# Gate and up products of a transformer block's MLP by Strassen's scheme: seven products over half tiles in place of eight

## The chip, the cores and the metric

The kernel runs on one NeuronCore of one Trainium2 chip. The metric is the device time of one launch in microseconds (us); lower is better. The kernel before took 2897.82 us, the median of three runs (2895.48 to 2900.39).

The engines named below: PE (TensorE, matrix products into PSUM banks), DVE (VectorE), ACT (ScalarE), POOL (GpSimd) and SP (SyncE, which here only issues DMAs). Each works off its own queue in order and waits on semaphores for the others.

## The reference, cut to what matters

```python
def _A_ref(x, wqkv, wo):          # B=1, S=2048, D=576, H=32 heads of 18
    ...
    p = _softmax(scores, axis=-1)
    ...
def _B_ref(x, w_gate, w_up, w_down):   # 576 -> 4608 -> 576
    g = jnp.einsum("bsd,df->bsf", x, w_gate)
    u = jnp.einsum("bsd,df->bsf", x, w_up)
    h = _gelu(g) * u
    return jnp.einsum("bsf,fd->bsd", h, w_down)

x = A_x
h = x + _A_ref(_layernorm(x, axis=-1), A_wqkv, A_wo)
h2 = h + _B_ref(_layernorm(h, axis=-1), B_w_gate, B_w_up, B_w_down)
```

All inputs are float32. The kernel computes products of float32 matrices from float16 parts: each operand is a high and a low part, and a product is high x high + low x high + high x low, so three float16 matmuls for each 128 rows of the contraction.

## The kernel before, in words

**Attention.** The first half, up to about 1560 us, is attention in units of four heads and 512 query rows, numbered n = 0 to 31, with 16 steps (kt) each. Row maxima run on DVE ahead of the exponentials on ACT. In the last three units, when the maxima run out, two generators are stepped beside the attention: `fill` multiplies the attention output by `wo` for one block of 512 rows (`wo_block`, L675), normalizes those rows and splits them into float16 parts, and `turn` (L231) transposes the parts into `XT` by DMA; `side` prepares the first weights of the MLP.

**MLP.** The width of 4608 is worked off in nine chunks of 512. `XT` holds the normalized rows, transposed: the 576 rows of the contraction are four tiles of 128 (high in `xh`, low in `xl`) and a tail of 64, whose high and low parts share one tile (`xt`). So one output tile of 128 wide by 512 rows takes 4 x 3 + 2 = 14 matmuls with 512 moving columns (`products`, L264, `accumulate`, L273). `gate_up` (L745) does that for gate and for up, for four tiles of the width and for one block of rows. ACT applies gelu out of the gate's bank (L756), DVE multiplies with the up bank (L759), ACT rounds to a high part (L760), DVE takes the low part (L761). `down` (L765) then multiplies the 512 wide hidden tile by the chunk of `w_down` in groups of 12 matmuls with 288 moving columns, and DVE adds each group onto `nat` (L779). Four PSUM banks serve the gate and up tiles, four the groups of `down`.

**Weights.** While chunk c is multiplied, the three pieces of chunk c+1 are loaded (`load_gate_up`, `load_down`: six and one DMAs on SP), their largest magnitudes are found (`exponents`, L113 on: DVE reduces over the free axis, PE transposes the column of 128 maxima at L131, DVE reduces again at L133, PE spreads the result over all partitions at L138), a power of two is made of it, and ACT and DVE split the weights into high and low parts (L252, L255, L739, L740). Two slots hold the split weights of two chunks. The loads have their own float32 buffers (`gf`, `uf`, `df`).

**Order of the work.** Up to the end of attention the order on PE, ACT, DVE and POOL is the program's own (`manual_schedule`), and generators are stepped with `take`. After `in_order.close()` (L865) a scheduler places the instructions of the MLP; the order on each engine is fixed at build time either way.

Of the kernel before, what the change touches and what calls it, by code (L numbers as in the profile page):

```python
# [2 lines left out]

# [14 lines left out]
P = 128  # L18
# [12 lines left out]
def tile_block(  # L31
# [27 lines left out]
    FT = 4  # L59
    FC = FT * P  # L60
    NCH = DF // FC
    QK = 2 * D
# [19 lines left out]
    down_ring = ring(singles)  # L82

# [32 lines left out]
    def exponents(views, name):  # L116
# [3 lines left out]
        ac = small.tile([P, n, k], F32, tag=f"ac{n}", name=f"ac_{name}")  # L120
# [67 lines left out]
    def rstd_of(t0, nt, root=False):  # L188
# [16 lines left out]
        for k in (1024.0,) if root else (1.0, 1.0, 1024.0):  # L205
# [463 lines left out]

    GU = 2 * 4 * (NK + 1) * FC  # L670
    xbs = [view(A, GU + 4 * HALF * i, (HALF,)) for i in range(3)]
    y = view(WK, 2 * 4 * TB * NPE, (D,))
    ys = [view(V, GU + 4 * FT * D + 2 * L * i, (L,), F16) for i in range(2)]

    def wo_block(b):  # L675

        for t in range(b * TPB, (b + 1) * TPB):
            for i in range(2):
                ws = slice(i * HALF, (i + 1) * HALF)
                xb = xbs[(2 * t + i) % 3]  # L680
                nc.sync.dma_start(xb, xv[:, t, ws])
                pt = next(m_ring)
# [5 lines left out]
        rstd_of(b * TPB, TPB)  # L688
        for t in range(b * TPB, (b + 1) * TPB):
            normed(y, nat[:, t], t)  # L690
            if b == 0:
                split_rows(ys[t % 2], y, nc.gpsimd.tensor_copy, nc.gpsimd.tensor_sub)
            else:
                split_rows(ys[t % 2], y, nc.vector.tensor_copy if b < NB - 1 else nc.scalar.copy)
            turn(ys[t % 2], t)
            yield


    slots = []
    for region in (V, W):  # L700
        t = [view(region, 2 * (NK + 1) * FC * i, (NK + 1, FC), F16) for i in range(4)]
        t += [view(region, GU + 2 * FT * D * i, (FT, D), F16) for i in range(2)]
        slots.append(t)
    hts = [[view(WK, 2 * FT * TB * (2 * i + k), (FT, TB), F16) for k in range(2)]
           for i in range(2)]
    ghost = {"h": 0}
    gf = view(A, 0, (NK + 1, FC))
    uf = view(A, GU // 2, (NK + 1, FC))
    df = view(V, GU + 4 * FT * D, (FT, D))

    def load_gate_up(c, eng=nc.sync):
        fs = slice(c * FC, (c + 1) * FC)
        load_w(gf, w_gate[:, fs], eng)
        load_w(uf, w_up[:, fs], eng)

    def split_gate_up(c, hi_on=None):

        gh, gl, uh, ul, _, _ = slots[c % 2]
        e = yield from exponents([gf, uf], "gu")
        s = pow2(e, -1, 268, "s_gu")  # L720
        gsc = pow2(e[:, 0:1], 1, -24, "gsc")
        hsc = pow2(e[:, 0:1], -1, 224, "hsc")
        yield from split_w(gf, s[:, 0:1], gh, gl, hi_on)
        yield from split_w(uf, s[:, 1:2], uh, ul, hi_on)
        return e, gsc, hsc

    def load_down(c, eng=nc.sync):
        eng.dma_start(df, w_down[c * FC : (c + 1) * FC, :].rearrange("(c p) n -> p c n", p=P))

    def split_down(c, e):  # L730

        dh, dl = slots[c % 2][4:]
        ed = yield from exponents([df], "dn")
        s = pow2(ed, -1, 268, "s_dn")
        nc.vector.tensor_add(ed, ed, e[:, 0:1])
        nc.vector.tensor_add(ed, ed, e[:, 1:2])
        dsc = pow2(ed, 1, -262, "dsc")
        for f in range(FT):
            nc.scalar.activation(dh[:, f], df[:, f], AF.Copy, scale=s)  # L739
            nc.vector.scalar_tensor_tensor(dl[:, f], df[:, f], s, dh[:, f],  # L740
                                           op0=ALU.mult, op1=ALU.subtract)
            yield
        return dsc

    def gate_up(c, b, gsc, hsc):  # L745

        gh, gl, uh, ul, _, _ = slots[c % 2]
        sl = slice(b * TB, (b + 1) * TB)
        hh, hl = hts[ghost["h"] % 2]
        ghost["h"] += 1  # L750
        for f in range(FT):
            ws = slice(f * P, (f + 1) * P)
            pg, pu = next(single_ring), next(single_ring)
            run(accumulate(pg[:, :TB], [(q, a) for a, q in products(sl, gh, gl, ws)]))
            ga = small.tile([P, TB], F32, tag="tmp", name="ga", bufs=3)
            nc.scalar.activation(ga, pg[:, :TB], AF.Gelu_apprx_tanh, scale=gsc)  # L756
            yield
            run(accumulate(pu[:, :TB], [(q, a) for a, q in products(sl, uh, ul, ws)]))
            nc.vector.scalar_tensor_tensor(ga, pu[:, :TB], hsc, ga, op0=ALU.mult, op1=ALU.mult)  # L759
            nc.scalar.copy(hh[:, f], ga)  # L760
            nc.vector.tensor_sub(hl[:, f], ga, hh[:, f])  # L761
            yield
        return hh, hl

    def down(c, b, h, dsc):  # L765
        hh, hl = h
        dh, dl = slots[c % 2][4:]
        for i in range(TPB):
# [140 lines left out]
```

## Time and profile before

| | us |
|---|---|
| median of three runs | 2897.82 |
| lowest, highest | 2895.48, 2900.39 |
| span of the profiled execution | 2899.4 |
| PE busy, share of the span | 2752.8, 95% |
| DVE busy | 1942.0, 67% |
| ACT busy | 1432.5, 49% |
| POOL busy | 321.8, 11% |
| largest group of the first half: row maxima on DVE (L532) | 1265.0 |
| products with 512 moving columns (L278), x2240 and x2044 | 491.4, 447.4 |

The only time of the profiled execution that the profile states is its span; it is 1.6 us above the median of the runs. In the rows of the profile "x" is the number of instructions, "busy" their time together, "mean ns" the time of one. Matmuls overlap in the pipeline, so the mean of one matmul is longer than the distance between two of them. A row of the timeline gives start and length in us, and in brackets how long the engine had been idle and who released it. "SPq" is SP's queue, where DMAs are issued.

### The profile page before, as it was taken

Reading aid. Unit: us, or ns where it says so; the run is one execution under the profiler, and the core shown is the slowest. Engines: PE = TensorE matmul, PEld = TensorE weight load, DVE = VectorE, ACT = ScalarE, POOL = GpSimd, SP = SyncE. Lnnn points to the kernel's source line nnn. Section 1 sums busy time; section 2 is a strip of 40 time slices with the busy share of each in tenths; the row PEclk is TensorE's granted clock in tenths of the full one; section 3 lists DMA queues with packets and bytes.
Section 4 is the critical chain, followed back from the end, with each engine's and each line's share of the span. In section 5 each row is a group of like instructions: output and inputs, shape, how many; then the busy total and the mean of one; then the engine's idle time right before and its main releaser. Section 6 shows DMA issues by size and latency. Waiting matters only on the chain.

```text
span 2899.4 us, 42932 instructions
## 1 busy us (share of the span) xinstructions
PE 2752.8 (95%) x17178; PEld 1152.0 (40%) x17178; DVE 1942.0 (67%) x3485; ACT 1432.5 (49%) x1626; POOL 321.8 (11%) x484
## 2 busy tenths in 40 slices
PE   7999999999999999999887999999999999999999
PEld 3542222222222222222223555555555555555555
DVE  6369999999999999999864725252525252524222
ACT  4217888888888888888563312121212121212111
POOL 2102421222212221212100000000000000000000
PEclk9999999999999999999998999999999999999999
DMA  8211110101001010101113301010101010100001
GB/s 216 67 58 39 40 35 14 38 14 32 14 18 34 14 38 12 35 14 50 40 45 93 96 1 53 1 53 1 53 1 53 1 53 1 53 1 1 1 17 50
DMA packets 109404, 105.08 MB, mean 36 GB/s; under 512 B 61780, under 2 KB 79828, under 8 KB 109204
## 3 DMA queue, kind: packets, MB, share of 16 engines
q1 hardware_dynamic: 102964, 89.98, 11.0%
q0 software_dynamic: 5712, 11.19, 1.4%
q8 instruction: 134, 2.20, 0.3%
q10 hardware_dynamic: 528, 1.18, 0.1%
q14 instruction: 66, 0.54, 0.1%
HBM read 72.09 MB, written 14.42 MB: 30 GB/s over the span
## 4 chain that ended last, share of the span: by engine, by line
PE 50%; DVE 43%; ACT 3%; DMA 2%; issue 1%; SPq 1%; POOL 0%; POOLq 0%; DVEq 0%; ACTq 0%
DVE mx L532 40%; PE pair L278 32%; PE bank L278 16%; PE bank L582 1%; PE bank L529 1%; ACT W L252 1%; ACT V L252 1%; DMA X<-V 0%; ACT V L739 0%; PE pair L576 0%; ACT W L739 0%; DMA X<-A 0%; ACT WK L578 0%; DMA A<-qk_hi 0%; DVE st L185 0%
## 5 line engine op out<-in xcount | busy, mean ns | idle before, releaser
L532 DVE TENSOR_REDUCE mx<-bank 128x1 f32<-128x512 f32 x2048 | 1265.0, 683 | 28.6 <-PE bank L529 28.5
L578 ACT ACTIVATE WK<-pair,p_ex_sc 128x1024 f32<-128x1024 f32 x1024 | 1084.6, 1113 | 235.8 <-PE pair L576 234.8
L582 PE MATMUL bank<-WK,V 128*32 128x512 f32 x4096 | 549.7, 608 | 0.1
L278 PE MATMUL pair<-X,V 128*128 128x512 f16 x2240 | 491.4, 381 | 8.8 <-ACT ga L756 8.6
L278 PE MATMUL pair<-X,W 128*128 128x512 f16 x2044 | 447.4, 379 | 1.5 <-ACT ga L756 1.5
L759 DVE SCALAR_TENSOR_TENSOR ga<-pair,p_hsc,ga 128x512 f32<-128x512 f32 x144 | 107.8, 749 | 506.3 <-PE pair L278 500.6
L278 PEld LDWEIGHTS <-WK 128*128 128x128 f16 x3456 | 338.1, 98 | 93.8 <-issue 0.5
L756 ACT ACTIVATE ga<-pair,p_gsc 128x512 f32<-128x512 f32 x144 | 98.8, 686 | 483.4 <-PE pair L278 483.4
L278 PEld LDWEIGHTS <-W 128*128 128x128 f16 x2296 | 223.7, 98 | 284.5 <-issue 13.6
L529 PE MATMUL bank<-W 54*128 54x512 f16 x1024 | 291.5, 382 | 43.1 <-DVE mx L532 14.1
L278 PEld LDWEIGHTS <-V 128*128 128x128 f16 x2240 | 219.4, 98 | 271.4 <-issue 14.8
L529 PE MATMUL bank<-A 54*128 54x512 f16 x1024 | 279.4, 382 | 36.0 <-DVE mx L532 6.1
L760 ACT CAST WK<-ga 128x512 f16<-128x512 f32 x144 | 88.9, 618 | 436.9 <-DVE ga L759 436.9
L779 DVE SCALAR_TENSOR_TENSOR nat<-bank,p_dsc,nat 128x288 f32<-128x288 f32 x288 | 147.7, 516 | 196.8 <-PE bank L278 196.8
L582 PEld LDWEIGHTS bank<-WK,V 128*32 128x32 f32 x4096 | 81.3, 108 | 434.4 <-issue 406.3
L278 PE MATMUL bank<-V,WK 128*128 128x288 f16 x1920 | 239.5, 286 | 0.2 <-DVE nat L779 0.2
L278 PE MATMUL bank<-W,WK 128*128 128x288 f16 x1536 | 191.4, 286 | 0.0
L576 PE MATMUL pair<-W 56*128 56x512 f16 x1024 | 159.3, 379 | 6.0 <-ACT WK L578 5.4
L576 PE MATMUL pair<-A 56*128 56x512 f16 x1024 | 156.5, 377 | 1.6 <-ACT WK L578 0.8
L761 DVE TENSOR_TENSOR WK<-ga,WK 128x512 f16<-128x512 f32 x144 | 99.3, 690 | 78.1 <-ACT WK L760 77.9
L605 POOL TENSOR_TENSOR rp<-rc,minus_one 128x16 f32<-128x16 f32 x28 | 81.9, 2924 | 616.3 <-DMA rc<-nat 616.3
L529 PEld LDWEIGHTS <-W 54*128 54x128 f16 x1024 | 59.3, 93 | 222.0 <-issue 220.0
(170 smaller groups left out, 1276.9 us busy)
## 6 DMA issues: line engine op xcount, KB each, us to landing
V<-in_B_w_down_dram SPq DMA_DIRECT2D x8, 1152.0 KB
nat<-rc SPq DMA_DIRECT2D x32, 256.0 KB
A<-in_B_w_gate_dram SPq DMA_DIRECT2D x8, 1024.0 KB
A<-in_B_w_up_dram SPq DMA_DIRECT2D x8, 1024.0 KB
qk_hi<-qk SPq DMA_DIRECT2D x36, 128.0 KB
qk_lo<-qk SPq DMA_DIRECT2D x36, 128.0 KB
A<-in_A_x_dram SPq DMA_DIRECT2D x32, 144.0 KB
out_dram<-nat SPq DMA_DIRECT2D x16, 288.0 KB
```

The costliest lines, as they stand in the source:

```text
L278: nc.tensor.matmul(dst, a, b, start=(i == 0), stop=(i == len(pairs) - 1))
L529: nc.tensor.matmul(pms[j][:, :TB], Q[r, q0 : q0 + P], K[r, kc * TB : (kc + 1) * TB], start=True, stop=True)
L532: nc.vector.tensor_reduce(mx[:, t, 2 * pr + j, kc : kc + 1], pms[j][:, :TB], axis=AX.X, op=ALU.max)
L576: nc.tensor.matmul(pS[:, j, :TB], K[r, kt * P : (kt + 1) * P], Q[r, qc * TB : (qc + 1) * TB], start=True, stop=True)
L578: nc.scalar.activation(pes[(2 * kt + pr) % NPE], pS[:, :, :TB], AF.Exp, scale=ex_sc)
L582: nc.tensor.matmul(acc[32 * hh : 32 * hh + 32, :TB], Vg[n // NB][:, kt * G4 + hh * VC : kt * G4 + hh * VC + 32], pes[(2 * kt + hh // 2) % ...
L605: nc.gpsimd.tensor_tensor(rc, den, minus_one.to_broadcast([P, R]), op=ALU.pow)
L756: nc.scalar.activation(ga, pg[:, :TB], AF.Gelu_apprx_tanh, scale=gsc)
L759: nc.vector.scalar_tensor_tensor(ga, pu[:, :TB], hsc, ga, op0=ALU.mult, op1=ALU.mult)
L760: nc.scalar.copy(hh[:, f], ga)
L761: nc.vector.tensor_sub(hl[:, f], ga, hh[:, f])
L779: nc.vector.scalar_tensor_tensor(nat[:, t, ws], pt[:, :HALF], dsc, nat[:, t, ws], op0=ALU.mult, op1=ALU.add)
```

## The change

Strassen's scheme (in Winograd's form) multiplies two matrices that are cut in halves both ways with seven products of halves in place of eight, at the price of sums of halves before and after. Here the weights of 576 by 256 are cut into four pieces of 288 by 128 (A11, A12, A21, A22, with the sums S1 to S4), and the rows of two blocks of 512 by 576 into four pieces of 512 by 288 (B11, B21, B22 and B12, with the sums T1 to T4). Per pair of width tiles and pair of row blocks, for gate and for up, seven products of 7 matmuls each (288 = 2 x 128 + 32: 2 x 3 matmuls, and one for the tail of 32, whose three part products are stacked in 96 rows) replace eight halves of 7 matmuls.

What goes with it:

- Chunks are 256 wide; there are 18, taken in pairs (`sc`), with one `w_down` piece of 512 by 576 per pair. A `unit(c, p)` is one chunk and one pair of row blocks: 14 products (seven for gate, seven for up, in turn), with the banks of one product continued by another. Besides gelu, multiply, high and low, DVE adds (L892, L896, L915, L920, L934, L939) and ACT copies banks to temporaries (two for each sum), so a unit has 14 operations on DVE and 14 on ACT for its four hidden tiles; before, four tiles had 8 and 8.
- `pair_rows` makes the 35 half pieces (five per piece: two high, two low, one tail) of a pair of blocks: DVE normalizes, POOL forms T1 to T4, DVE casts and subtracts, and SP transposes 35 tiles by DMA for each 128 rows. Pair 0 is made beside the last attention units, pair 1 beside the first `down`, there with one buffer for all parts. The splitting of rows in `wo_block` is gone.
- Weights of one matrix at a time go through one float32 buffer `W8` (8 pieces of 288 by 128), loaded by ten DMAs; POOL forms S1 to S4; `exponents` is run for each matrix, so 36 times, and nine times for `w_down`.
- The six banks of a unit leave two banks for everything else: `down`'s groups, and the transposes and spreads of `exponents`, take turns on one ring of two (`down_ring = m_ring`).
- The order of the whole MLP is now the program's own on PE, ACT, DVE and POOL: `beside(main, side)` steps the weight preparation after each product or group of the main work, by two steps and by one in turn. SP's order is still the scheduler's.

```diff
+    def pair_rows(p, region, off, parts_of):
+        F7 = view(region, off, (7, HALF))
+        B22, B11, B21, T1, T2, T3, T4 = (F7[:, i] for i in range(7))
...
+        for i in range(TPB):
...
+            for q, (o0, o1) in enumerate(((0, 4), (4, 7))):
...
+                nc.vector.tensor_copy(r[:, :, :M2], f[:, :, :M2])
...
+                yield
+                nc.vector.tensor_sub(r[:, :, M2 : 2 * M2], f[:, :, :M2], r[:, :, :M2])
...
+                for a, b in ((0, 9), (9, 18), (18, 35)):
...
+                    nc.sync.dma_start_transpose(dst, rows[:, (a - k0) * P : (b - k0) * P])
+                yield
...
+    def split_matrix(c, m, hi_on=None):
+        wh, wl = slots[c % 2][m]
+        nc.gpsimd.tensor_add(W8[:, S1], W8[:, A21], W8[:, A22])
...
+        e = yield from exponents([view(A, W8O + 4 * 4 * KT * P, (2, 2 * KT * P))], f"m{m}")
+        nc.vector.tensor_copy(ee[:, m, c % 2 : c % 2 + 1], e)
+        s = pow2(e, -1, 266, f"s_m{m}")
+        for a, b in ((4, 7), (0, 4)):
...
+                nc.scalar.activation(wh[:, a:b], W8[:, a:b], AF.Copy, scale=s)
...
+            yield
+            nc.vector.scalar_tensor_tensor(wl[:, a:b], W8[:, a:b, :2], s, wh[:, a:b, :2],
                                            op0=ALU.mult, op1=ALU.subtract)
             yield
+            r = slice(2 * KR, 3 * KR)
+            nc.vector.scalar_tensor_tensor(wh[r, a:b, 2], W8[r, a:b, 2], s[r], wh[r, a:b, 2],
+                                           op0=ALU.mult, op1=ALU.subtract)
+            yield
...
+    banks = [singles[0], singles[1], singles[2], pairs2[0][:, 0], pairs2[0][:, 1], pairs2[1][:, 0]]
...
+    def unit(c, p):
...
+        xg, xu = next(tmp_ring), next(tmp_ring)
+        product(0, g[0], A11, B11, True)
+        nc.scalar.copy(xg, g[0])
+        yield
+        product(1, u[0], A11, B11, True)
+        nc.scalar.copy(xu, u[0])
+        yield
+        product(0, g[1], A12, B21, True)
+        nc.vector.tensor_add(xg, g[1], xg)
+        yield
+        product(1, u[1], A12, B21, True)
+        gelu(xg, xg)
+        nc.vector.tensor_add(xu, u[1], xu)
+        gate(xg, xu)
+        yield
...
+        product(1, u[2], S4, B22, False)
+        nc.vector.tensor_add(au, u[2], au)
+        gate(ag, au)
+        high(0, 1, ag)
+        low(0, 1, ag)
+        yield
...
+    down_ring = m_ring = ring([singles[3], pairs2[1][:, 1]])
...
+    def beside(main, side, every=2):
+        for i, _ in enumerate(main):
+            take(side, 1 + (i % every == 0))
...
+    for sc in range(NCH // 2):
...
+        if sc:
+            run(nxt[0])
+            beside(unit(c, 0), side)
+        run(nxt[1])
+        beside(unit(c + 1, 0), side)
+        run(nxt[2])
+        dsc = kept.pop()
+        if sc == 0:
+            side = pair_rows(1, A, MAT, [view(A, MAT + 4 * 7 * HALF, (4 * 5 * P,), F16)] * 2)
+        beside(down(0, dsc, last), side)
+        run(side)
...
+        run(unit(c, 1))
+        nxt = [] if last else [split_chunk(c + 2), split_chunk(c + 3), keep(split_down(sc + 1))]
+        side = chain(*nxt)
+        beside(unit(c + 1, 1), side)
+        beside(down(1, dsc, last), side)
```

The order of the instructions at three places. First, PE where the maxima of new weights are transposed (L131, after: L132) and spread (L138, after: L139) beside the groups of `down`. Before:

```order
L278 MATMUL bank_71<-V,WK 128x288
L131 MATMUL bank_69<-id_78,am_gu 1x128 x2
L131 MATMUL bank_68<-id_78,am_dn 1x128
L278 LDWEIGHTS W
L278 MATMUL pair_66<-X,W 128x512
...
L278 MATMUL pair_66<-X,W 128x512
L138 MATMUL bank_70<-a_gu,ones 128x2
L138 MATMUL bank_69<-a_dn,ones 128x1
L278 LDWEIGHTS W
```

After, in the second `down` of a pair of chunks, for the up matrix of the next chunk (`a_m` is DVE's result from the transposed column):

```order
L279 MATMUL bank_71<-W,WK 128x288
L132 MATMUL pair_67<-id_78,am_m_21826 1x128
L139 MATMUL bank_71<-a_m_21857,ones 128x1
L279 LDWEIGHTS WK
L279 MATMUL pair_67<-W,WK 128x288
```

Five matmuls stood between transpose and spread before; at this place nothing stands between them now, and the groups of `down` on both sides use the same two banks.

Second, DVE where the next `w_down` is measured (`ac_dn`, `am_dn`: maxima of the columns and of the matrix). Before, with the gate weights' maxima (`ac_gu`) ahead of it:

```order
L124 TENSOR_REDUCE ac_gu<-A 128x1 x3
L124 TENSOR_REDUCE ac_dn<-V 128x1
L127 TENSOR_REDUCE am_gu<-ac_gu 128x2
L124 TENSOR_REDUCE ac_dn<-V 128x1 x2
L759 SCALAR_TENSOR_TENSOR ga<-pair_67,p_hsc,ga 128x512
L124 TENSOR_REDUCE ac_dn<-V 128x1
L761 TENSOR_TENSOR WK<-ga,WK 128x512
L127 TENSOR_REDUCE am_dn<-ac_dn 128x1
```

After, in the unit before the first `down` of a pair of chunks (the rows ahead end the previous unit):

```order
L800 SCALAR_TENSOR_TENSOR W<-A,p_s_m_18793,W 128x1024
L934 TENSOR_TENSOR V<-bank_70,V 128x512
L882 TENSOR_TENSOR WK<-tmp,WK 128x512
L804 SCALAR_TENSOR_TENSOR W<-A,p_s_m_18793,W 32x4x128
L939 TENSOR_TENSOR W<-pair_67,W 128x512
L876 SCALAR_TENSOR_TENSOR V<-W,p_hsc_18360,V 128x512
L882 TENSOR_TENSOR WK<-V,WK 128x512
L892 TENSOR_TENSOR WK<-bank_69,WK 128x512
L125 TENSOR_REDUCE ac_dn<-A 128x1 x2
L896 TENSOR_TENSOR V<-pair_66,V 128x512
L876 SCALAR_TENSOR_TENSOR WK<-V,p_hsc_18709,WK 128x512
L125 TENSOR_REDUCE ac_dn<-A 128x1 x2
```

The maxima are taken soon after the last low part of the up matrix (L804), and the load of `w_down` between the two goes into the buffer that L804 has just read; the unit's own sums stand behind the maxima.

Third, SP where row parts are transposed. Before, the last block of rows:

```order
L231 DMA_TRANSPOSE X<-V 128x9x128
L238 DMA A<-in_B_w_gate_dram 64x512
L236 DMA A<-in_B_w_up_dram 128x4x512
L231 DMA_TRANSPOSE X<-V 128x9x128 x2
```

After, the first of four rounds for pair 1, and the next:

```order
L748 DMA_TRANSPOSE X<-A 128x9x128 x2
L748 DMA_TRANSPOSE V<-A 128x2x128
L748 DMA_TRANSPOSE V<-A 128x15x128
L748 DMA_TRANSPOSE X<-A 128x9x128 x2
L748 DMA_TRANSPOSE V<-A 128x2x128
```

A block of 128 rows took 9 tiles; a pair of them takes 35 now, in two lots of 20 and 15 tiles out of one buffer.

More of the change, by code (lines that the diff above doesn't have):

```diff
@@ L2 @@
 from contextlib import ExitStack
+from itertools import chain
 import concourse.bass as bass
@@ L711, in load_gate_up @@
[L711 to L725, printed above, removed]
```

345 lines of the change are left out of this document (231 added, 114 removed).

## The prediction

> **What bounds the kernel now.** I read the page's engine times and its slices first, then the MLP by windows, the chunk period on SP's queue, and the groups of one period by form. From 1660 us on PE never stops:
>
> ```profile
> PE 2752.8 (95%) x17178; PEld 1152.0 (40%) x17178; DVE 1942.0 (67%) x3485; ACT 1432.5 (49%) x1626; POOL 321.8 (11%) x484
> 1800.00:1900.00 100.00, 100.00 (x574) 55.92 (x573) 27.39 (x44) 15.65 (x24) 0.00 (x0) 1.00 0.00 1
> 1900.00:2000.00 100.00, 99.61 (x565) 55.03 (x563) 45.88 (x92) 23.82 (x37) 0.00 (x0) 1.00 0.12 39
> ```
>
> (Columns: window, its length, busy time of PE, PEld, DVE, ACT, POOL, granted clock, DMA share, GB/s.) PE is busy 99.6 to 100 of 100 us at full clock, DVE 27 to 46. Only fewer matmuls shorten this stage, and DVE has room on average. The next rows give the period of a chunk, the distance of matmuls and the prices of DVE and ACT work.
>
> ```profile
> 1765.62 0.37 SPq L236 DMA_DIRECT2D A<-in_B_w_gate_dram  x1
> 1766.28 0.48 SPq L237 DMA_DIRECT2D A<-in_B_w_gate_dram  x1
> 1766.81 0.59 SPq L238 DMA_DIRECT2D A<-in_B_w_gate_dram  x1
> 1910.86 0.37 SPq L236 DMA_DIRECT2D A<-in_B_w_gate_dram  x1
> 1752.14 0.52 DVE L779 SCALAR_TENSOR_TENSOR nat<-bank,p_dsc,nat 128x288 f32<-128x288 f32 x1 [0.95 <-PE bank L278]
> 1753.61 0.52 DVE L779 SCALAR_TENSOR_TENSOR nat<-bank,p_dsc,nat 128x288 f32<-128x288 f32 x1 [0.95 <-PE bank L278]
> 1780.94 0.69 ACT L756 ACTIVATE ga<-pair,p_gsc 128x512 f32<-128x512 f32 x1 [1.59 <-PE pair L278]
> 1786.99 0.69 ACT L756 ACTIVATE ga<-pair,p_gsc 128x512 f32<-128x512 f32 x1 [1.35 <-PE pair L278]
> ```
>
> A chunk of 512 takes 1910.86 - 1765.62 = 145.24 us. Two gelus are 28 matmuls apart: 6.05 / 28 = 0.216 us for one with 512 columns. Two evictions are a group of 12 apart: 1.47 us. So 448 x 0.216 + 32 x 1.47 = 96.8 + 47.0 = 143.8; the remaining 1.4 is the transposes and spreads of `exponents`.
>
> ```profile
> L759 DVE SCALAR_TENSOR_TENSOR ga<-pair,p_hsc,ga 128x512 f32<-128x512 f32 x16 | 12.0, 748 | 55.6 <-PE pair L278 55.6
> L761 DVE TENSOR_TENSOR WK<-ga,WK 128x512 f16<-128x512 f32 x16 | 11.0, 689 | 8.2 <-ACT WK L760 8.2
> L760 ACT CAST WK<-ga 128x512 f16<-128x512 f32 x16 | 9.9, 618 | 48.9 <-DVE ga L759 48.9
> L124 DVE TENSOR_REDUCE ac_gu<-A 128x1 f32<-128x512 f32 x10 | 6.2, 669 | 0.0
> L124 DVE TENSOR_REDUCE ac_dn<-V 128x1 f32<-128x576 f32 x4 | 2.9, 736 | 0.0
> L252 ACT ACTIVATE W<-A,p_s_gu 128x512 f16<-128x512 f32 x6 | 3.8, 710 | 12.9 <-DVE p_s_gu L170 12.9
> L739 ACT ACTIVATE V<-V,p_s_dn 128x576 f16<-128x576 f32 x4 | 2.8, 766 | 0.0
> L255 DVE SCALAR_TENSOR_TENSOR W<-A,p_s_gu,W 128x512 f16<-128x512 f32 x5 | 3.4, 745 | 0.0
> L740 DVE SCALAR_TENSOR_TENSOR V<-V,p_s_dn 128x576 f16<-128x576 f32 x4 | 3.0, 806 | 0.0
> L617 POOL TENSOR_TENSOR nat<-nat 128x512 f32<-128x512 f32 x31 | 39.5, 1274 | 273.6 <-DMA nat<-rc 236.3 <-ACT WK L578 30.6 <-ACT A L152 6.7
> 1774.00:1776.00 2.00, 2.00 (x11) 0.93 (x10) 2.00 (x5) 0.69 (x1) 0.00 (x0) 1.00 1.06 295
> ```
>
> By the two lengths of each (64 elements are 67, 56 and 61 ns), I estimate for the new shapes: maximum of 768 0.94 us (0.87 behind another), ACT on 1152 and 1536 1.27 and 1.6, DVE's low parts of 768, 384, 1024 and 512 about 0.95, 0.55, 1.2 and 0.67 in a queue, a sum, multiply or low of 512 0.7. (The last two rows are a POOL operation and a window in which weights were loading.)
>
> **Matmuls.** The order shows 3528 products with 512 columns in the MLP for 4032 before: 392 per pair of chunks, 84.7 us. With `down` unchanged a period is 131.7 bare, 12.1 under the 143.8 before; nine times that is 109 us. The rest of the sum is what eats it.
>
> **The preparation in a fixed order.** DVE and ACT get 14 operations each per unit, 14 x 0.7 = 9.8 us of a unit's 14 x 1.51 = 21.2. A unit with preparation carries about 9 us more on DVE, so DVE is 0.9 full, in order, with ACT in between; whatever it is late, PE meets at a transpose or at a bank. I walked the queues through one period; three places carry the stalls. POOL's four sums of 384 per matrix, 4 x 1.0 us by its row of 512, cost nothing: ACT asks for them six products or groups after the load, 9 us; without that cover a matrix would wait 1 to 2 us on ACT, and the bank copies behind it.
>
> *w_down's maxima.* In the unit before, the up matrix's scale is ready 16.3 us in; then follow ACT 1.27, a bank copy 0.6, sum and multiply 1.4, low parts 0.95 + 0.55, low and multiply 1.4, low part 1.2, sum and low 1.4, low part 0.67: 25.8, while PE left at 22.8. So 3.0 us into the next unit the buffer is free for `w_down`. Its load takes 5.9 (issue and first byte about 0.9, 4.0 for 1.18 MB at the window's 295 GB/s, 1 to land: an estimate), the first two maxima end at 10.2, the unit's own sum and multiply stand between and take 1.4, the last maxima end at 13.1. PE is there after six products, 9.1. Stall 4.0.
>
> *The second `down`.* The last low part of the unit waits for sum, multiply and ACT's high part, and ends 4.1 us after PE has begun; the first eviction ends at 4.6. With two banks the third group wants its bank at 2.9: 1.7. Two maxima (1.8), an eviction and the small maximum end at 7.0; the third group is through at 6.1: 1.0 at the transpose. The spread stands right behind it and waits for DVE's reduction, 0.6; the second matrix of this `down` adds 0.8 and 0.3. Together 4.4.
>
> *Elsewhere:* 0.5 at the first transpose, 0.9 at a bank copy that stands behind a weight activation on ACT, 1.1 at the first `down`'s banks, 0.3 in small ones: 2.8. Own time of five transposes and spreads, by the 1.4 above: about 2.0.
>
> *Clock.*
>
> ```profile
> 1568.00:1569.00 1.00, 0.75 (x4) 0.23 (x3) 0.61 (x2) 0.00 (x0) 0.00 (x0) 1.00 0.65 131
> 1570.00:1571.00 1.00, 0.00 (x0) 0.00 (x0) 0.00 (x0) 0.00 (x0) 0.00 (x0) 1.00 0.04 7
> 1571.00:1572.00 1.00, 0.00 (x0) 0.00 (x0) 0.00 (x0) 0.00 (x0) 0.00 (x0) 0.52 1.11 212
> 1580.00:1581.00 1.00, 1.00 (x3) 0.29 (x2) 0.00 (x0) 0.00 (x0) 0.00 (x0) 0.50 0.16 61
> 1581.00:1582.00 1.00, 1.00 (x5) 0.44 (x4) 0.63 (x1) 0.00 (x0) 0.00 (x0) 0.86 0.00 0
> 1575.54 21.11 PE L278 MATMUL pair<-X,V 128*128 128x512 f16 x84 [6.79 <-ACT ga L756]
> ```
>
> PE stopped at 1568.75; from 1571 the clock was half, and until 1581.2, 5.7 us after work had begun again: 2.9 us lost. The stall of 4.0 is longer than the 2.3 us it took to fall, so I count 2.0 per period (bounds 0 and 2.9). [...]
>
> A period is then 131.7 + 2.0 + 4.0 + 4.4 + 2.8 + 2.0 = 146.9, 1.7 over 145.2. Eight periods are like this: +14; the last has no preparation in its last unit and `down`: -5.
>
> **Pair 1 of the rows, beside the first `down`.**
>
> ```profile
> 1562.08 2.15 SPq L231 DMA_TRANSPOSE X<-V  x1
> 1565.07 5.93 SPq L231 DMA_TRANSPOSE X<-V  x3
> 1437.31 10.05 SPq L231 DMA_TRANSPOSE X<-V  x4
> 1565.79 0.46 DVE L226 CAST V<-WK 128x576 f16<-128x576 f32 x1 [1.18 <-DMA X<-V]
> 1566.28 0.69 DVE L227 TENSOR_TENSOR V<-WK,V 128x512 f16<-128x512 f32 x1
> ```
>
> Nine tiles take 2.0 to 2.5 us on the queue, so 0.25 us a tile; the cast that had to wait for the first transpose began 3.7 us after its issue, so about 1.45 pass from the queue's end to DVE. With one buffer a round of 128 rows is serial: cast and low part of four pieces 2.4, 20 tiles 6.45, of three pieces 2.0, 15 tiles 5.2, together 16; four rounds 64. The evictions of `down` stand behind the waiting casts on DVE, so PE goes with them: 64 for 16 x 1.47 + 1.1 = 24.6, so +39.5. Bounds: the tiles alone, 140 x 0.22 = 31, so +6; 0.28 a tile and a slower landing, +50. The rest of this period: bare 131.7, own 1.2, `down`s and stalls 7.3, clock after the long wait 2: 181.7 for 145.2, +37.
>
> **Around the end of attention.**
>
> ```profile
> 1438.54 0.58 PE L529 MATMUL bank<-W 54*128 54x512 f16 x1 [6.51 <-DVE mx L532]
> 1444.26 0.58 PE L529 MATMUL bank<-W 54*128 54x512 f16 x1 [1.46 <-DVE mx L532]
> 1562.69 0.59 ACT L596 COPY nat<-bank 128x512 f32<-128x512 f32 x1 [1.20 <-issue]
> 1581.37 0.69 DVE L621 TENSOR_TENSOR nat<-nat 128x512 f32<-128x512 f32 x1 [3.73 <-DMA nat<-rc]
> 1589.51 0.70 SPq L635 DMA_DIRECT2D X<-nat  x1
> 1562.53 6.22 PE L278 MATMUL pair<-X,V 128*128 128x512 f16 x28
> ```
>
> Block 0 is no longer split beside unit 29, where PE waited 6.5 and once more 1.5: -8. Pair 0 is made in units 30 and 31, when the maxima are over and DVE has room; its 140 tiles share SP with the attention's row transfers (bounds -7 and +20; I take 0, since the row blocks 1 and 2 had their transposes there too). After attention the last rows must come back through DRAM before `wo_block(3)`: before, they landed about 1592 (1589.5, 0.7 and a landing), and PE filled the time with 28 + 84 matmuls but for 6.8 and the slow clock. Now only seven products (10.6) stand ahead: from 1562.5 to 1573, and with transposes and a `w_down` load out of the way I take 1587 for the landing: 14 idle, 2 of clock, 6 for the up matrix of chunk 1, which nothing covers, for about 12 lost before: +10. Together +2.
>
> **Sum.** +14 - 5 + 37 + 2 = +48 on the span of 2899.4: 2947. The span lies 1.6 above the median, within the spread of the runs, so I leave the sum as it is.
>
> **Rivals.** *The preparation stays hidden.* DVE is 0.9 full in two units of six stages only; if sums, copies and waits are quicker than their nearest rows, PE loses little. With 1.5 of stalls and no clock drop: 8 x (131.7 + 2.0 + 1.5 - 145.2) = -80, with +37 and +2: 2858. It decides where stalls and clock together are under 7.1 us per period for my 13.2. Against it: the transposes stand at fixed places, and the chain to w_down's maxima has no slack in it.
> *Two clock drops per period.* The three stalls of the second `down` (1.7, 1.0, 0.6 within 7 us) may do it too; 2.9 x 9: 2973.
> *Late loads.* A matrix comes with ten DMAs instead of three; at 0.59 each, (1766.81 + 0.59 - 1765.62) / 3, SP issues for 5.9 us. I gave most of it cover, since the buffer's four inputs are free before the sums are. If not, 2 us for each of four matrices: 8 x 8 = +64, 3011. [...]
> *Pair 1 at the pace of its tiles:* -31, 2916.
> That the products are not fewer is excluded by the order.
>
> **Chances and range.** Forecast 0.46 (2925 to 2970), hidden preparation 0.15, two drops 0.17, late loads 0.10, pair 1 hidden 0.12. The range 2870 to 3010 leaves out the far halves of the first and third rival. A measurement tells 0.2%, about 6 us, from no change: faster 0.16 (hidden preparation and a little of pair 1), within 0.04, slower 0.80.
>
> **What would show it.** After: a chunk pair of about 147 us between loads of one kind in steady state; PE idle before the w_down transposes (L132, `am_dn`) of about 4 us each, eight times, with the clock at 0.5 behind; about 64 us for the first `down` with DVE casts (L729) waiting for DMA; L868 3528 times. Wrong would be a period near 135 or above 153, or a first `down` under 35 us.

## The result

The changed kernel takes 2965.88 us (median, 2962.95 to 2966.57) where the kernel before, beside it, takes 2899.11: a ratio of 1.0231, 95% interval 1.0217 to 1.0246. It is slower by 67 us; 2947 was predicted, within 2870 to 3010. The profiled span is 2963.7 for 2899.4.

The engine times of the changed kernel's page:

```profile
PE 2697.1 (91%) x16755; PEld 1110.7 (37%) x16755; DVE 2247.1 (76%) x4068; ACT 1590.2 (54%) x1826; POOL 524.8 (18%) x683
```

PE is busy 56 us less than before (2752.8) and the span is 64 longer. The loads of `w_down` on SP's queue mark one pair of chunks each; the first three of the nine and the last:

```profile
1626.56 0.38 SPq L822 DMA_DIRECT2D A<-in_B_w_down_dram  x1
1809.39 0.39 SPq L822 DMA_DIRECT2D A<-in_B_w_down_dram  x1
1957.39 0.39 SPq L822 DMA_DIRECT2D A<-in_B_w_down_dram  x1
2846.08 0.39 SPq L822 DMA_DIRECT2D A<-in_B_w_down_dram  x1
```

From 1809.39 to 2846.08 are seven periods of 148.1 us, for 145.24 before; the first one takes 182.8. One steady period as a window (columns as in the prediction), and PE's stops of 0.25 us and more in it:

```profile
1957.39:2105.61 148.22, 138.91 (x794) 77.45 (x792) 90.06 (x176) 47.38 (x68) 18.99 (x17) 0.99 0.10 28
1961.00 2.74 PE L868 MATMUL pair<-X,W 128*128 128x512 f16 x7 [2.06 <-ACT V L889]
1969.96 1.02 PE L868 MATMUL pair<-X,W 128*128 128x512 f16 x4 [0.25 <-DVE ab_dn L141]
1984.89 1.63 PE L279 MATMUL bank<-W,WK 128*128 128x288 f16 x12 [1.06 <-DVE nat L958]
2036.52 0.27 PE L132 MATMUL bank<-id,am_m 128*1 128x128 f32 x1 [0.59 <-DVE am_m L128]
2038.86 1.02 PE L868 MATMUL pair<-X,W 128*128 128x512 f16 x4 [0.25 <-DVE ab_m L141]
2051.19 0.42 PE L279 MATMUL bank<-W,WK 128*128 128x288 f16 x2 [0.47 <-ACT WK L879]
2052.25 0.30 PE L279 MATMUL bank<-W,WK 128*128 128x288 f16 x1 [0.64 <-DVE WK L882]
2052.84 1.63 PE L279 MATMUL pair<-W,WK 128*128 128x288 f16 x12 [0.30 <-DVE tmp L939]
2055.51 1.63 PE L279 MATMUL bank<-W,WK 128*128 128x288 f16 x12 [1.03 <-DVE nat L958]
2057.71 0.27 PE L132 MATMUL pair<-id,am_m 128*1 128x128 f32 x1 [0.58 <-DVE am_m L128]
2058.53 0.38 PE L139 MATMUL bank<-a_m,ones 1*128 1x1 f32 x2 [0.55 <-DVE a_m L136]
2074.71 0.27 PE L132 MATMUL pair<-id,am_m 128*1 128x128 f32 x1 [0.67 <-DVE am_m L128]
2077.06 1.63 PE L279 MATMUL bank<-W,WK 128*128 128x288 f16 x12 [0.30 <-DVE nat L958]
2097.91 0.59 PE L868 MATMUL pair<-V,W 128*128 128x512 f16 x2 [0.41 <-ACT W L918]
```

PE stands still for 148.22 - 138.91 = 9.3 us of this period, where before it stood still for 0.4 of one (144.85 busy of 145.24). No stop is long: one of 2.06 at the first bank copies of a unit, and many of 0.3 to 1.1, most of them around the second `down` (2051 to 2077). Everywhere it is DVE's or ACT's result that comes last.

In this period the clock falls behind the stop of 2.06 (seven matmuls in 2.74 us), as in three of the seven. In the other four PE stands still for 10.5 to 10.7 us: behind the same stop they have two more, which the slower matmuls cover here.

```profile
2402.06:2550.09 148.03, 137.38 (x794) 77.05 (x792) 90.09 (x176) 47.49 (x68) 19.16 (x17) 1.00 0.10 28
2409.52 1.67 PE L868 MATMUL pair<-V,W 128*128 128x512 f16 x7 [0.67 <-DVE V L896]
2411.89 0.38 PE L132 MATMUL bank<-id,am_dn 128*1 128x128 f32 x2 [0.70 <-DVE am_dn L128]
```

In the first period SP's transposes of pair 1 come in four rounds (the first, second and last begin here), and PE goes with them:

```profile
1660.28 2.79 SPq L748 DMA_TRANSPOSE X<-A  x2
1663.11 6.67 SPq L748 DMA_TRANSPOSE V<-A  x2
1674.52 2.73 SPq L748 DMA_TRANSPOSE X<-A  x2
1702.92 2.76 SPq L748 DMA_TRANSPOSE X<-A  x2
1666.41 3.04 PE L279 MATMUL pair<-W,WK 128*128 128x288 f16 x12 [6.75 <-DVE nat L958]
1680.68 3.04 PE L279 MATMUL pair<-W,WK 128*128 128x288 f16 x12 [5.84 <-DVE nat L958]
1694.82 3.04 PE L279 MATMUL pair<-W,WK 128*128 128x288 f16 x12 [5.75 <-DVE nat L958]
1706.33 3.17 PE L868 MATMUL bank<-X,A 128*128 128x512 f16 x7 [5.09 <-DMA X<-A]
```

A round is 14.2 us; DVE's cast waits about 5 us in each for the transposes of the buffer that it writes, with the evictions of `down` behind it. After each of these stops the row of a group of twelve is 3.04 us long instead of 1.63.

### The profile page after: what moved, and what is told of

The parts are those of the page before. It is cut to its first block, busy times and chain, and to the rows that moved or that the text cites. A ratio compares the mean times of both kernels' runs of the same rounds, so it can differ in the third digit from the quotient of the medians.

```text
span 2963.7 us, 43958 instructions
## 1 busy us (share of the span) xinstructions
PE 2697.1 (91%) x16755; PEld 1110.7 (37%) x16755; DVE 2247.1 (76%) x4068; ACT 1590.2 (54%) x1826; POOL 524.8 (18%) x683
## 4 chain that ended last, share of the span: by engine, by line
DVE 55%; PE 35%; ACT 4%; DMA 3%; issue 2%; SPq 1%; POOL 0%; DVEq 0%; ACTq 0%; POOLq 0%
DVE mx L533 39%; PE pair L279 9%; PE bank L279 9%; PE bank L868 8%; PE pair L868 7%; DVE WK L882 2%; DVE ac_m L125 1%; ACT WK L879 1%; DMA A<-in_B_w_down_dram 1%; DVE nat L958 1%; DVE W L844 1%; DVE tmp L876 1%; DVE W L800 1%; PE bank L583 1%; DMA X<-A 1%
## 5 line engine op out<-in xcount | busy, mean ns | idle before, releaser
L868 PEld LDWEIGHTS <-W 128*128 128x128 f16 (+1 forms) x2394 | 234.2, 98 | 317.0 <-issue 50.0
L279 PE MATMUL bank<-W,WK 128*128 128x288 f16 x1824 | 253.6, 287 | 29.9 <-DVE nat L958 20.3
L279 PE MATMUL pair<-W,WK 128*128 128x288 f16 x1632 | 226.4, 289 | 21.7 <-DVE nat L958 18.3
L868 PE MATMUL pair<-X,W 128*128 128x512 f16 (+1 forms) x792 | 221.6, 384 | 22.2 <-ACT tmp L889 10.3
L868 PE MATMUL pair<-V,W 128*128 128x512 f16 (+1 forms) x720 | 203.1, 380 | 8.5 <-ACT tmp L918 3.0
L796 ACT ACTIVATE W<-A,p_s_m 128x1152 f16<-128x1152 f32 (+1 forms) x52 | 72.6, 1412 | 198.2 <-DVE p_s_m L171 198.2
L958 DVE SCALAR_TENSOR_TENSOR nat<-bank,p_dsc,nat 128x288 f32<-128x288 f32 x152 | 78.3, 515 | 97.9 <-PE bank L279 95.8
L530 PEld LDWEIGHTS <-A 54*128 54x128 f16 x1024 | 56.7, 93 | 208.7 <-issue 205.3
L958 DVE SCALAR_TENSOR_TENSOR nat<-pair,p_dsc,nat 128x288 f32<-128x288 f32 x136 | 70.0, 515 | 81.3 <-PE pair L279 80.0
L868 PEld LDWEIGHTS <-A 128*128 128x128 f16 x882 | 86.2, 98 | 108.2 <-DMA X<-A 5.4
```

The lines of the kernel that those rows point to most:

```text
L279: nc.tensor.matmul(dst, a, b, start=(i == 0), stop=(i == len(pairs) - 1))
L530: nc.tensor.matmul(pms[j][:, :TB], Q[r, q0 : q0 + P], K[r, kc * TB : (kc + 1) * TB], start=True, stop=True)
L796: nc.scalar.activation(wh[:, a:b], W8[:, a:b], AF.Copy, scale=s)
L868: nc.tensor.matmul(bank, w, x_, start=start and i == 0, stop=i == len(mm) - 1, skip_group_check=not start)
L958: nc.vector.scalar_tensor_tensor(nat[:, t, ws], pt[:, :HALF], dsc, nat[:, t, ws], op0=ALU.mult, op1=ALU.add)
```

## The experiments

Theory A: the seven products save what they promise, and two things eat it: weight preparation that PE meets unready in every period, and the serial rows of pair 1 once. Its rivals are named with each run. In all tables of periods below the period is the mean distance of the `w_down` loads in steady state (for the first run, of the evictions of two `down`s).

**Without preparation.** The weights of the first pair of chunks serve all later ones.

```diff
-        dsc = kept.pop()
+        dsc = kept[0]
...
-        nxt = [] if last else [split_chunk(c + 2), split_chunk(c + 3), keep(split_down(sc + 1))]
+        nxt = [iter(())] * 3
```

> Leaves out the preparation of all weights after the first pair of chunks (no loads, sums, maxima, transposes, spreads, scaling), so every pair of chunks multiplies by the first pair's weights. Theory A (the preparation beside the products is what eats their saving): the period of a pair falls from 148.1 to the bare 131.7 plus about 1 for banks, so 8 x 15.4 = 123 off, about 2842 us, and PE idle under 1.5 us per period. Theory B (the units lose time by themselves, at their own sums, copies and banks): the period stays above 140 and the time above 2900.

Measured: 2850.06 us (2845.59 to 2852.33). One period as a window, from the first eviction of one `down` to that of the next but one:

```profile
1824.70:1957.90 133.20, 132.20 (x777) 75.72 (x776) 55.16 (x89) 34.07 (x56) 0.00 (x0) 1.00 0.00 1
```

133.2 us, PE idle 1.0. The units alone lose little: theory B falls. Bare, the period is 145.2 - 133.2 = 12.0 us under that of the kernel before, which has its preparation in it (1.4 by the prediction's count), and the new preparation costs 148.1 - 133.2 = 14.9.

**Without the maxima.** The scales found for the first pair are used again; loads, sums, scaling and low parts stay.

```diff
+        if steady[0]:
+            for _ in range(n * k + 3):
+                yield
+            return held[name]
```

> Leaves out the maxima of weights after the first pair of chunks with their transposes and spreads (the scales measured first are used again); loads, sums, scaling and low parts stay, at the same places. Theory A (most of the 14.9 us that the preparation costs per period comes of PE meeting fresh maxima and of the DVE time they take): period 137 to 140, 8 x 9.5 = 76 off, about 2890 us. Theory F (the scaling and low parts crowd ACT and DVE and delay banks and evictions): period 143 or more, 2925 us or more.

Measured: 2902.57 us (2897.01 to 2906.05; ratio 1.0019, 1.0009 to 1.0028). The period is 139.7, so the maxima with their transposes and spreads cost 8.4 of the 14.9, and DVE is busy 77 us of a period instead of 90. The larger part is theirs, as theory A said (its 2890 us were 13 too low), but 6.5 stay, and so does the longest stop, unchanged, although no maximum is taken any more:

```profile
1941.81:2081.44 139.63, 133.60 (x778) 75.51 (x776) 76.97 (x140) 47.37 (x68) 18.98 (x17) 1.00 0.10 30
1945.41 1.67 PE L878 MATMUL pair<-X,W 128*128 128x512 f16 x7 [2.06 <-ACT V L899]
```

**One step at a time.**

```diff
-            take(side, 1 + (i % every == 0))
+            take(side)
```

> The preparation takes one step after each product or group instead of one and two in turn: 52 steps over 58 places instead of about 35. Theory A (DVE and ACT are too full in the stretch with preparation, and PE meets their lateness): the PE idle of a period falls from 9.2 to about 4, and the restarts with it, so a period of about 142 and 8 x 6 = 48 off, about 2918 us. Theory C (each transpose, spread and load costs PE the same wherever it stands): period 147 to 149, 2955 to 2970 us.

Measured: 3081.57 us (ratio 1.0633, 1.0615 to 1.0651), period 162.0: slower by 116. The expectation rested on a wrong count. A pair has four matrices of 16 steps and a `w_down` of 16, 80 steps, not 52. At 58 places one by one they don't come through, and what is left is run at once ahead of the unit that needs it. PE then waits for a matrix that has just been asked for, and for `w_down`'s scaled parts:

```profile
1973.86 0.37 PE L132 MATMUL bank<-id,am_m 128*1 128x128 f32 x1 [9.40 <-DVE am_m L128]
2003.18 0.28 PE L279 MATMUL bank<-W,WK 128*128 128x288 f16 x1 [2.14 <-ACT W L843]
```

So the run tells nothing between theories A and C. It shows that the changed kernel's pace (87 steps' room for 80) has hardly any slack.

**Four banks for `down`.** The groups of `down` use four of the six banks of the unit that is over.

```diff
-    down_ring = m_ring = ring([singles[3], pairs2[1][:, 1]])
+    m_ring = ring([singles[3], pairs2[1][:, 1]])
+    down_ring = ring([banks[1], banks[4], banks[2], banks[5]])
```

> The groups of down take turns on four banks of the unit that is over, the transposes and spreads keep their two for themselves. Theory A (the two shared banks cost about 3 us in the second down of a period, and 1 in the first): 8 x 3 to 4 off, about 2936 us. Theory D (the evictions are late because DVE is, and PE only waits at the next transpose instead): under 8 us off, 2956 to 2966 us.

Measured: 2971.79 us (ratio 1.0249, 1.0234 to 1.0264), period 148.8: no gain, if anything a loss. PE no longer waits for evictions in the second `down`, and so it arrives earlier at the transpose and waits there for all of it. The stop at the transpose, the group behind it, and a window of 1 us in that group:

```profile
2061.09 0.27 PE L132 MATMUL bank<-id,am_m 128*1 128x128 f32 x1 [2.23 <-DVE am_m L128]
2062.53 2.89 PE L279 MATMUL pair<-W,WK 128*128 128x288 f16 x12 [0.25 <-DVE ab_m L141]
2063.00:2064.00 1.00, 1.00 (x6) 0.60 (x4) 0.00 (x0) 0.00 (x0) 0.00 (x0) 0.50 0.00 0
```

Several small waits (1.03 for an eviction, then 0.58) have become one of 2.23, 0.55 and 0.25 in a row, and the clock falls to half behind it. Over seven periods the granted clock is 0.97 where it was 1.00 (changed kernel first, then this one):

```profile
1810.00:2850.00 1040.00, 967.22 (x5551) 541.04 (x5550) 633.07 (x1229) 334.04 (x480) 132.60 (x119) 1.00 0.10 29
```

```profile
1810.00:2850.00 1040.00, 978.92 (x5539) 548.92 (x5538) 627.94 (x1223) 331.10 (x476) 132.98 (x119) 0.97 0.09 28
```

PE is idle 12 us less in them, and busy 12 us more at the same work. The wait moves to the next transpose, as theory D said; that the clock falls too was in neither theory, and the time lies above D's 2956 to 2966.

**Own buffers for pair 1.** Seven pieces of row parts get a place each, in three buffers (four, one and two pieces).

```diff
-            side = pair_rows(1, A, MAT, [view(A, MAT + 4 * 7 * HALF, (4 * 5 * P,), F16)] * 2)
+            side = pair_rows(1, A, MAT, [view(A, PB, (4 * 5 * P,), F16),
+                                         view(A, PB + 8 * 5 * P, (5 * P,), F16),
+                                         view(V, 4 * PIECES * TB + 4 * TB, (2 * 5 * P,), F16)],
+                             ((0, 4), (4, 5), (5, 7)))
```

> The row parts of pair 1 go into three buffers (four pieces, one, two) instead of one for all, so the casts of the next lot wait only for their own buffer's transposes. Theory A (cast, transposes and landing in series through one buffer): a round falls from 14.2 us to the pace of its 35 tiles and a landing, 9 to 10, so about 18 off, 2946 us, and PE's three waits of about 6 us fall to about 2. Theory E (DVE's evictions behind the casts, or the transposes' own pace, hold PE anyway): under 5 us off.

Measured: 2957.3 us (2951.89 to 2959.52), 8.6 less than the changed kernel. The second and third round, and PE's last stop:

```profile
1674.72 2.72 SPq L748 DMA_TRANSPOSE X<-A  x2
1684.13 2.69 SPq L748 DMA_TRANSPOSE X<-A  x2
1696.83 3.17 PE L868 MATMUL bank<-X,A 128*128 128x512 f16 x7 [10.65 <-DMA X<-A]
```

Rounds take 9.4 us instead of 14.2 and the first period 167.5 instead of 182.8: one buffer was the cause of the serial rounds. The time lies between the theories. The stops inside `down` shrink to 1.8 at most, but half of what is won there comes back as one of 10.65 behind it, since the next unit needs the last transposed tiles. (The profiled execution is 10 us shorter, not 15: it reached the first load of `w_down` 5 us later, in a part whose code is the same in both.)

**The preparation one unit earlier.** The first gate matrix of the next pair is loaded, summed and measured in the unit that had no preparation, with a step between the maxima and the transpose and one between transpose and spread; the second run adds the own buffers.

```diff
-        run(unit(c, 1))
         nxt = [] if last else [split_chunk(c + 2), split_chunk(c + 3), keep(split_down(sc + 1))]
         side = chain(*nxt)
+        for i, _ in enumerate(unit(c, 1)):
+            if i < 10 + 2 * lag[0]:
+                take(side)
```

> The preparation of the next pair begins one unit earlier, in the unit that had none (the first gate matrix is loaded, summed and measured there; its scaling waits for the slot as before), and one step each lies between the maxima and the transpose and between the transpose and the spread. Theory A: PE no longer meets a transpose or spread whose input is not ready, but the DVE stays as full in the rest; PE idle of a period 9.2 to about 4, period about 142, 8 x 6 = 48 off, about 2918 us. Theory F (crowding by scaling and low parts): under 15 off, 2951 us or more.

> The earlier preparation and the three buffers for the row parts of pair 1 together. If the two causes lie in different stages they add: the result of the earlier preparation less 9 (the buffers alone gave 8.6), about 2909 us; if the buffers' gain only moves a wait, no more than 3 below the earlier preparation alone.

Measured: 2939.63 us (ratio 1.0153, 1.0137 to 1.017) and 2924.9 (1.0097, 1.0082 to 1.0112). The period is 144.6 in both, 3.5 less than 148.1: between the theories. The stops at transposes and spreads are gone but for one (0.99), while those for banks and evictions in the second `down` grew to 1.7. The run moves start and steps at once, so it doesn't tell which of them did it. The buffers shorten the first period by 15 here as they did alone (177.1 to 161.8, and 182.8 to 167.5): the two causes lie in different stages and add.

**The scheduler's order.** Nothing is moved by hand; only, the loop over pairs is left to the scheduler on all engines, as the MLP was before.

```diff
     side = chain(*nxt)
+    in_order.close()
     for sc in range(NCH // 2):
...
-    in_order.close()
```

> The loop over pairs of chunks is ordered by the scheduler on all engines, as the MLP of the kernel before was, instead of in the program's order. Theory A (PE stands still because a fixed order puts the transposes and banks ahead of matmuls that could run): period about 143, 8 x 5 = 40 off, about 2925 us. Theory G (the waits come of two banks and of DVE's queue in any order): within 10 of the changed kernel, 2956 to 2976 us; a worse order would show as over 2976.

Measured: 2890.51 us (2886.45 to 2894.8): 75 less than the changed kernel, and 0.28% faster than the kernel before (ratio 0.9972, 0.9963 to 0.9982). The period is 139.5, the first one 166.9. A steady period and PE's stops in it:

```profile
1935.53:2075.00 139.47, 136.62 (x794) 76.99 (x793) 89.16 (x176) 47.29 (x68) 18.75 (x17) 1.00 0.10 30
1939.74 1.67 PE L868 MATMUL pair<-X,W 128*128 128x512 f16 x7 [0.87 <-ACT V L889]
1962.15 1.63 PE L279 MATMUL bank<-W,WK 128*128 128x288 f16 x12 [0.46 <-DVE nat L958]
2027.53 0.30 PE L279 MATMUL bank<-W,WK 128*128 128x288 f16 x1 [0.56 <-DVE WK L882]
```

The same work, with DVE just as full (89 us), the same two banks and the same buffers, and PE is idle 2.9 us instead of 9.3 to 10.7. What differs on PE at the place where transpose and spread of the up matrix stood back to back in the second `down` (order of this kernel):

```
L132 MATMUL pair_67<-id_78,am_m_16152 1x128
L868 LDWEIGHTS A
L868 MATMUL bank_68<-X,A 128x512
...
L868 MATMUL bank_68<-X,A 128x512
L279 LDWEIGHTS WK
L279 MATMUL pair_67<-W,WK 128x288
L139 MATMUL bank_71<-a_m_16183,ones 128x1
```

Four matmuls of the next unit and one of `down` lie between them; in the program's order there was nothing. On DVE the last two maxima of `w_down` stand apart, with one of the unit's own operations between, and the maxima of the four matrices are done 2.4 to 51 us before PE transposes them; in the program's order it is 0.05 to 0.3. The order changed on all engines at once, so the run doesn't separate PE's from DVE's. Theory A as this run put it had expected 40 of these 75 (16 of them lie in the first period, of which it did not speak); theory G falls.

**On top of the scheduler's order.** The three helpers again, now in that order.

> The scheduler's order for the loop and the three buffers for pair 1. In the scheduler's order the PE stop behind the first down is still 19.75 us, on the last transposes of four serial rounds of 13.3. Theory A (one buffer makes the rounds serial in any order): rounds of about 9.3, 12 to 16 off the 2890.5 of the scheduler's order alone, about 2877 us. Theory E (the landing of the last round is what counts): under 5 off.

> The same and the preparation one unit earlier with a step of slack behind the maxima and the transpose. Theory A (what is left of the 139.5 us period over the 133.2 without preparation is PE meeting late inputs): 2 to 4 per period off, 2877 - 8 x 3 = about 2853 us. Theory G (the scheduler already places matmuls into these gaps, so the earlier start has nothing left to give, or costs by other conflicts): 2872 to 2885 us.

> The scheduler's order, the three buffers, and four banks for the groups of down beside the two of the transposes and spreads. Theory D (two shared banks still stop down where evictions are late, and in the scheduler's order PE has other work when it gets through): 2 per period off, 2877 - 16 = about 2861 us. Rival (the banks of the unit that is over are also those that the next unit's products need early, so the scheduler loses overlap between down and unit): 2877 or more.

| scheduler's order with | time, us (range) | ratio to before, 95% | period |
|---|---|---|---|
| own buffers | 2878.24 (2871.57 to 2882.99) | 0.9933 (0.9920 to 0.9947) | 139.2 |
| own buffers, earlier preparation | 2865.48 (2863.19 to 2868.1) | 0.9887 (0.9872 to 0.9901) | 137.3 |
| own buffers, four banks | 2865.11 (2862.82 to 2867.49) | 0.9888 (0.9875 to 0.9901) | 137.6 |

The first and the third came out as their first theory said. The earlier preparation won 1.9 of a period, just under its theory A, and its time lies between the two theories. The four banks are worth noting: in the program's order they won nothing (6 slower, with intervals that overlap), in the scheduler's 13.

**Together,** with the scheduler's order from the end of attention on:

```diff
+    in_order.close()
     it = unit(0, 0)
```

> All that helped in one kernel: three buffers for pair 1, preparation one unit earlier, four banks for down, and the scheduler's order, here from the end of attention on instead of from the loop on. If the earlier preparation (12.8 off beside scheduler and buffers) and the four banks (13.1 off) take away different waits, they add: about 2852 us without the transition; theory G (both remove the same waits, of which only about 2 us per period are left): 2860 to 2866. The transition (from the last attention matmuls to the first w_down load, about 69 us now with some 14 of PE waits): 5 to 10 less if the scheduler fills the waits for transposes, none if the chains of DVE behind wo's last block set it.

Measured: 2845.9 us (2844.82 to 2850.84), ratio 0.9827, 0.9813 to 0.984: the best version, 1.7% faster than the kernel before. The period is 136.7, 0.6 to 0.9 under either helper alone, where 1.6 and 1.9 would have come off if they added: these two remove the same waits for the larger part, nearer to theory G. The rest came from the transition: from the last copy of attention (ACT) to the first load of `w_down` it is 54.3 us (1560.60 to 1614.90) where the kernel with the earlier preparation has 69.1 (1566.15 to 1635.21) and the one with own buffers 66.3, so more than the 5 to 10 expected.

```profile
1560.60 0.59 ACT L603 COPY nat<-bank 128x512 f32<-128x512 f32 x1 [1.20 <-POOL V L717]
1614.90 0.39 SPq L828 DMA_DIRECT2D A<-in_B_w_down_dram  x1
1899.46:2036.31 136.85, 135.25 (x793) 77.29 (x792) 87.27 (x176) 47.78 (x68) 17.37 (x17) 1.00 0.11 31
1671.40 3.17 PE L874 MATMUL bank<-X,A 128*128 128x512 f16 x7 [14.55 <-DMA X<-A]
```

What is left: PE idle 1.6 us a period, the transposes' and spreads' own time, and once 14.55 us for the last rows of pair 1.

## Why the prediction was right, and where it was not

*Products.* Right. The bare period was put at 131.7, with a 1.1 for banks beside it; without preparation 133.2 was measured, with PE busy for 132.20. The 12.1 saved were counted against 143.8, the period before without transposes and spreads; against that the measured 133.2 saves 10.6.

*Own time of transposes and spreads, 2.0.* Too small. In the version with everything together PE is busy 135.25 in a period, without preparation 132.20: at most 3.0, since its few stops add to the busy time too.

*w_down's maxima, a stall of 4.0 at the transpose.* Too large, and with a cause left out. DVE does wait for the load (up to 2.2 us), but PE had already stopped for 2.06 us earlier in the unit, at a bank whose copy (ACT L889) stood behind the late end of the previous unit. So in the four periods without a clock drop 0.67 is left behind DVE's maxima, 0.70 at the transposes and 0.25 at the spread, 1.6 for the 4.0; in the period shown first, with a drop, only the 0.25. Together with the 2.06 that is 3.7, near to the 4.0 by chance: the run without maxima shows that the 2.06 isn't theirs. It stays there, and is gone without any preparation (PE idle 1.0). The walk had a bank copy under "elsewhere", at 0.9, but behind a weight activation; here ACT waited for DVE.

*The second `down`, 4.4.* Right in size and place: from 2051.19 to 2058.53 the rows add up to 3.57, and the second matrix has 0.67 and 0.30, together 4.5.

*Elsewhere, 2.8.* 0.59, 0.25, 1.06 and 0.41 are 2.3.

*Clock, 2.0 per period.* Wrong. The granted clock falls in three of the seven periods; in windows of 20 us from 1800 to 2860 what is missing to 1.00 comes to about 5 us in all, 0.7 a period. And little of it shows in the time: the three periods with a drop take 148.22, 148.52 and 148.03 us, the four without one 147.93 to 148.03, since the slower matmuls cover waits that follow. What the working left out in its place is that a stop costs more than its idle time. The row of a group of twelve is 1.63 us long, but in a stream the next group begins after 1.47 (2077.06 and 2078.53), because the last matmul overlaps the next. Before a stop nothing overlaps it, so each stop counts some 0.16 more, as busy time (the profile models where a matmul ends). For the 16 stops of a period without a drop that is an estimate of 2.6; they have 137.4 of busy time where the version that hardly stops has 135.25.

*The period.* 146.9 predicted, 148.1 measured. The idle time was 9.3 to 10.7 where the three stalls made 11.2; the clock took less than its 2.0, and the stops' ends and own time took more. That the sum came so near is partly errors that cancel.

*Pair 1.* 181.7 predicted and 182.8 measured for the period; four serial rounds of 14.2 for the 16 predicted, and a stop of 5.09 at the first product behind them that the working did not have. With it the first `down` takes 57.5 us (from PE's first group at 1648.88 to that product) for the 64 of the working, so the rest of the period was put some 8 too low, and the match is partly luck. The run with own buffers shows the mechanism, one buffer. Its +37 is the larger half of the loss: 182.8 - 145.2 = 37.6.

*Around the end of attention, +2.* Half wrong. Unit 29 became 6.6 shorter (8 predicted) and unit 30 stayed, but unit 31 takes 72.4 us for 64.4. PE waits there for the first gate matrix, whose maxima stand behind pair 0's casts on DVE, 10.43 us where it waited 7.62 before. And it waits 4.60 and 8.60 for rows of the attention output (X<-nat), 2.55 and 5.34 before; SP has pair 0's transposes between their transfers now. The first row is from before:

```profile
1508.98 0.59 PE L131 MATMUL bank<-id,am_gu 128*1 128x128 f32 x2 [7.62 <-DVE am_gu L127]
1501.04 0.37 PE L132 MATMUL bank<-id,am_m 128*1 128x128 f32 x1 [10.43 <-DVE am_m L128]
1619.12 0.37 PE L132 MATMUL bank<-id,am_m 128*1 128x128 f32 x1 [8.48 <-DVE am_m L128]
```

I had taken 0 for pair 0's cost between bounds of -7 and +20; +8 was in there. The uncovered up matrix of chunk 1, put at 6, is 8.48 (last row).

*The sum.* The span grew by 64.3 for +48: about 9 of the difference from the period (1.2 in each of seven or eight), 1 from the first, and about 5 from the end of attention, which came 2.8 earlier than before instead of 8. Of these 2.8, units 29 to 31 are 1.3 the other way; 4.0 came ahead of them, where the code is the same in both and its end varies between 1380.0 and 1385.1 among the runs.

*Rivals.* That the preparation stays hidden is excluded by the 14.9. Its point of decision, 7.1 us of stalls and clock, agrees with the scheduler's order, where 139.5 - 131.7 - 2.0 = 5.8 are left for them and the kernel is faster than before; but there the first period is 16 shorter as well, so the point isn't tested alone. Two clock drops per period did not occur, although their 2973 lies nearer to the measured time than the 2947 does; the four banks brought something like them. Late loads are excluded: in six periods DVE waits for no load of a gate or up matrix, only for `w_down` (12.1 us in six times, 2.2 at most), whose load was put at 5.9 us and took 5.7 (1957.39 to 1963.08). Pair 1 at the pace of its tiles did not occur with one buffer; with three it nearly does.

What the prediction did not see is where the choice lay. It named the fixed order as the place of the stalls, but took DVE's fullness (0.9) and the two banks as their cause. The scheduler's order has the same fullness and the same banks, and PE stands still for a third of the time (2.9 us for 9.3 and more): so the order decides, which put each result so close ahead of its use that PE met it late. How much of that is PE's order and how much DVE's and ACT's is not shown. The transposes and spreads are the smaller part of it: freed of their stops by the earlier preparation, the period falls by 3.5, and the scheduler's order takes off 8.6, most of the rest at banks and evictions.

## What to carry to other kernels

A saving in matmuls is only worth what the preparation beside it leaves, so price the preparation by leaving it out (14.9 us a period here, where the bare period is 12.0 shorter) before touching the arithmetic. Short waits that PE meets in a fixed order were cured here by an order that puts independent work between producer and consumer, not by more banks: without a change of order those brought nothing (2971.79 us for 2965.88). And one buffer that fed both a cast and a DMA made the rounds serial here (14.2 us each, 9.4 with three buffers): count cast, transfer and landing as one chain.

## What the runs showed of the hardware

The length of a stop alone did not settle whether the clock fell behind it. In the changed kernel the stop at the unit's first bank is 2.06 us in seven periods and 2.04 in an eighth, to 0.02 the same, yet the seven matmuls behind it take 1.67 us in five of them and 2.74, 1.95 and 2.71 in three. One of the five:

```profile
2109.22 1.67 PE L868 MATMUL pair<-X,W 128*128 128x512 f16 x7 [2.06 <-ACT tmp L889]
```

The three drops begin at 1961.44, 2258.40 and 2702.13 and last 3.41 us each, at half clock. The first of them, and a window of the same length over the seven matmuls of 2109.22, where the clock stays:

```profile
1961.44:1964.85 3.41, 3.41 (x10) 1.17 (x9) 1.77 (x3) 0.19 (x1) 0.00 (x0) 0.50 0.22 86
2108.21:2111.62 3.41, 2.40 (x12) 1.09 (x12) 1.57 (x4) 1.31 (x3) 0.00 (x0) 1.00 0.63 249
```

What sets the three stops apart from the five is left open. I had taken the clock's fall as a matter of length alone, and charged it to every period.
